# Three groups of transposes moved from TensorE to DMA, with a new order of the work, in an interleaved memory-transformer and gated-MLP kernel

## The chip, the cores and the metric

The kernel runs on one core of a Trainium2 chip. A core has five instruction streams that matter here: PE (TensorE, matmuls; its weight loads are shown apart as PEld), DVE (VectorE), ACT (ScalarE), POOL (GpSimd) and SP (SyncE, which issues all of this kernel's DMAs). The metric is the device time of one launch in microseconds (us). Before the change it is 1519.08 us, the median of three runs (1517.13, 1519.08, 1519.72).

## The reference

Input x has 2048 tokens of 448 numbers. Four layers are applied one after the other, each added to its input: A, B, A, B.

Layer A is attention with a recurrent memory. Its normalised input is cut into 64 segments of 32 tokens. Ahead of each segment stand 8 memory rows, so 40 rows are attended to at a time, by 16 heads of 256, with a mask that lets a token see the memory and the tokens up to itself. The first 8 rows of a segment's output are the memory of the next segment; this makes a chain of 64 steps that can't be done side by side.

```python
for s in range(n_seg):
    h = concat([mem, x[s*32:(s+1)*32]])          # 40 rows
    q, k, v = h @ Wq, h @ Wk, h @ Wv
    p = softmax(where(mask, q @ k.T * scale, -1e9))
    o = (p @ v) @ Wo
    mem, out_s = o[:8], o[8:]
```

Layer B is a gated MLP on the normalised rows: gate = x Wg, up = x Wu, h = relu(gate) · up, out = h Wd, with 1792 hidden numbers. The second A starts from the same initial memory and has the same weights as the first, and so have the two Bs.

## The kernel before

**Layout.** The tokens are worked on in 16 tiles of 128, four segments each. Wq and Wk are multiplied together ahead of time into A, and Wv and Wo into Bsb, so that a head's scores are h A h^T and its output is P h Bsb. All weights stay in SBUF. What flows between stages is bf16.

**The chain.** `chain(step)` does one memory step of both A layers at once: layer 1 runs seven steps (LAG) behind layer 0. Only the 8 memory rows of a segment go through it. Products with A (L885), turned on DVE (L1059, L1067), scores and softmax in `middle` (L1082 to L1100), P turned on PE (L1115) and copied to PTm, P times the rows (L1139, L1142, from HR), the product with Bsb (L926), and a split into two bf16 halves that puts the new memory rows back into mT, HT and HR. For layer 1 the rows for HR are four DMAs from Rsb on SP; for layer 0 they are copied.

**The riders.** In layer 1 the tokens of even tiles ride along in unused columns of the chain's matmuls, 16 of them a step (`ride`, and `third` near the end). Their softmax is a second call of `middle` with a mask, with its own Pr and PTr, of which there is one each. It is emitted behind the chain's step and its result is used by the next step's product. A rider's result goes by DMA from Rsb to Tsb, eight issues a step.

**The tokens.** `att_group` does a tile's tokens for a quarter of the heads, four calls a tile: products with A into Ug (L1228), scores (L1254), softmax on DVE and ACT (L1261 to L1267) into Px, two PE transposes (L1273) into a PSUM bank, one copy into PTx, P times the rows (L1139, L1142) into YT, and the product with Bsb (L1303). Layer 0 has all 16 tiles and layer 1 the eight odd ones: 96 calls. Px has two buffers, PTx one.

**The MLP.** `norm` normalises a tile's rows (L1159 to L1168) into xn and, for the MLP, turns them by four PE transposes (L1174) into a bank. From there one copy of 128x512 fills blocks 0 to 3 of G2, and two copies of 64x384 fill blocks 4 to 6 with the halves swapped. `glu_units` reads G2 in pairs of half-height matmuls (L1327), `glu_down` multiplies with Wd (L1346). There are 32 MLP tiles. The rows for layer A (`norm` with another destination) are turned the same way, into HT and HX.

**What sets the order.** The program is recorded as operations with their costs, and `_Sched` lays them out before anything runs. PE's order is written out: LINE lists, operation by operation, which of those not yet placed comes next, and PE does exactly that order. ORDER shifts the due times of parts of the work, which decides the order on the other engines. An operation waits on semaphores for what it reads; there is no other choice at run time. Each engine, SP among them, does its list in sequence. For a DMA the plan takes a cost on SP (750 or 640 ns), its bytes at 240 a nanosecond, and 1800 ns to land. A change of PE's tiling is planned at 94 ns (TURN). Where PE would stand idle long enough (L267), `filler` puts dummy matmuls (L1360) into a free PSUM bank.

Of the kernel before, what the change touches and what calls it, by code (L numbers as in the profile page):

```python
# [12 lines left out]
D = 448  # L13
# [5 lines left out]
L = SEG + M  # L19
# [13 lines left out]
ORDER = ("bpAIADoUQHoTkoMiV0AFwEKXLXJgtlHyqWXmIAyASPAYGXRWF0TArkrptiYIWoOAZasL0tFJGlTFY0Pedbealsyx0xoaZwia00qain0aZhAqaa"  # L33
         "cadkYaijdaUN0aD0m0aaUq0AqNQHxbPP0XcAhyv0bfDu0ZIrGH0UPaaaxbawMsAcXQyNBy0hi0mLLnTInmxTcmcobaXApXz0jagMaQLfnPpTIL"
         "HMxTAQTSZiNNblpydZg0geLAJizGtLa0jagUxTedmKDD0iU00msmturofpI0IAryFNTMkbTvuDpa0cls0MUtoc0ASOXN0DAs0FaRDazrtMsuoT"
         "0WNcIsHAPagayA0DOPTCQndFH0SANUPHki0MFvzaHuatOHNAbPqVt0qILltpAOehTTg00zngDSv0F0AaKNLAmrjWmTySi0muj0NXlaNd0KkAFJ"
         "TkhTraEYaAGBA0pDPTvfvtzKlo0oTAyaIsgQfHAye0jXsTgWNqGGXsAZadTaFYhmO00APvWovBKSASpAWILKnJPSlAaXUFk0xQMjLfnAXHQAKh"
         "tqfFLHPE0ieJ0wXdrkbWeTalAaoAbBwcdomWDzQPLNggtFrfiXWSsBOxTXKrAstuhHvQLCaZkaxNazRHeRhfqyLUHbrXTJgG0wJ0YEVDJTKnAV"
         "lC0PJXjpDrc0pD0ApoEmOmMwXxSREx0cxzoPOsmadeaLLAAj0piwNJ0lsyWbapNSJVVIsVOsihOZwYAW0jaRFtZbyCaqTaKNbJQTfIB0mZS0Cc"
         "WxgOQZcnsYWAoAITywNmqXZUhIPgkCkP0Jdz0ubAW0ZhAoPAcmjhqTtPaiVaJlb0KEBYgskpDe0DR0CWAAqQTsDKYTTAgjdedfcQPGPnAsAa0p"  # L40
         "avNPCvdomUwqVOJc0xauAvNdte00NPHjppXCUqsbyAAyNhifJMAXbzeWlwVjZXuELnDd0HVgTaAEafBwIEaRHujNotAXn00JAfBST0SeGqg0bi"
         "jwfrq0VssGFsaEjazUWQIpRMksFRCWhQNqSYNZMwWYXwgzxLmvPo0yhHRFerP0e0aIz0LUKmshQkGBgtIJulh0AAauQzacAadK0PyjGtjbaaaa"
         "aaAThZKZSaaaaaaaaaaaaaaaaaaawXLEBNvdaUYLxbEb")

SIGNS = "ABCDEFGHIJKLMNOPQRSTUVWXYZabcdefghijklmnopqrstuvwxyz0123456789+-*/=<>()[]{}.,:;!"
LINE = ("AEFAEDKLFHHDDEDEDMKIFGGEEDADCKJGFEEDDCCCJKIFGDCDCDMLCJAFEDEDCBBKIEGCCBBBBBKJ1DBGAEDBAAMAHOMCCBJBBCAAAdeAFbBMCA"
        "BWDVVADOCSCAPBbOABMfEAWKBVKJBBABBADYBARBAAVFBADVACNDACKBDPBADGGDNNDLEDEEDAFECAAAAAWAAAKARAAPHdAcGASAQAAAU~FBMA"
        "~CAhgA(ACdAAbA+aADXXXXDDAATEADDQPAAAALAAJJJAIIAHAGGABBDAABBAAAAAATMiAAXWdWKAaJJ~JALlAK~N~EKAAAEEAHDAZZGFCABFBS"
        "BBWQABOAAMMMAAKAJKKAzQJCIHHBGGGAFAHGADADJABBAAAAAACANBBYAXQAGIaISAHWAGAAARFDeEEAGCaZFFABBFBSBBQVAPBAAMMMAAKAJK"
        "K2AsQJCIHHBGGGAFoIHeBADEAACBBAEAAABCAAMBAYXQAJbbKTAhIAeAAAHERYADA--EiDpC6AEBB82DABEAxfEDuuuAAFrAEErqEmAlAlCAjo"  # L50
        "ShhKggg9BAfIdVACabaAAYAACAUZABSKAQQQDAANGOiPOgYBLMcrVMRAKKcKKKAgKDAHCCSFyyAfAPACsAARpBAn~DnnnD!EDAAiAhDjiDDAFA"
        "AcaAAZYC*BWAAAASSSAS0DQBSRAANOUAAALAJJDCHHHAHIGASGGAAOASACMBeVKBSBYBBBOFTAEAEDA.}Cut[CUC>A]pD/APCC999FAAK5A465"
        "lCCA1AA5AyCAwvmdtttBAb)FppBGnonEADDqjDDAmgCKeCdddCDbDDaaaZCPFWCbCALSARXAQQQTDZDDNAFAAI99EDGAAA3AA16jBzHyyyHyAW"
        "vALuuAsKAQpACOAlCBjnADhhhAAfBABAedbACACB4XAAAUATSmSSSASphBCAANAAaAKAlkDAbhIUmwUIISBAfTAFAAACKXBB1KKBBBFWFIBEAA"
        "><QEEC-CCCA7B-BH4AcBA000AZAxCwAxwCkBjUrBwBAonWmDBBBOhhhBBXfeBBddC9DbCgAZFXIWAVVVAAAVSpUU/n2SADRXAAPOWOBAMMMBOA"
        "KDJIJ54DVDGAAyADAv0DuMCsssABqACoppDNCFAAjJ>hhDAfDCAcccEcAAZABBYYAAATATpwSSAWsAQAPPPAAAMAaAKAdAArIUfATGGGaAPoAA"
        "DMMDALCAOBBBGZGYBIEB[[GKGACC/CA(ME9A8h777AA5BA65BbAi1zEAAXwAvukBBrrrsATYEnXmDnm9DRDjpDDDgDkeeDdddAAbcEbbBGBBXA"
        "DFaUASERAAPPPCRAAMA==CKuAIJA7HWW+4AN2M111MAYyBXAyxDOUDDqAAEvoBBmAlk,CBiiiAAhCAeABAccDACCXAAVAAZTASmSSSTAgnBAAA"
        "NAAZAAAjAIUAATdFRFFPRPAEAMACAJOBJTIBBBOWFBEFBA((EPDO/G)CCA9KAo6o5556CfCC1Aj00AADAAvC~BBUrrBquASoooCemAQnmQCBOB"
        "fBfBBAicAaaAZZZCAIWBXYXAHKSDSAAAPOCNRAMMMEAAKAIHA+9QPH6OAFb82FA0ZAyyyAfAvAAwvBKAJrxDoAAGmBk(kBKAhhhDhAgDCdAEAb"  # L60
        "aEDAAAAUAASnSuSSSASoACAAAALAZAJAkAAUHBBBVEEPhAXNdCCOLSYCAJBJcJBBBXJVBEASAC<=vFuE+CC=FABB4nBBBcAyA1AAvvv~GBAt~D"
        "AutsUAEpSuAAmdlDkkkBBiNBBfggEDeAAAbgCGYPXAEVVVBMBSUCRERRADgDBNTVBBLDAIIUCbCGGGPAAHFDDAgwwDNDAsABDIBnsAmNlllBLB"
        "iAJDfAffC}dCAiAaACAXAWA9AUUUAASARTSqAoRQBBOBNAMMMAALKAAeXjCiJVBVmeJIARrFTGdSAFaEE4OEEEAHZDACA][DACFC=AB)B-AA9L"
        "A7778AA5BAAA32bAAzC4AXwvdumtttlBuArqbtspFFnoZGAktqkFjEiiijEEiEfxFhhADDdIEibEEZFWhXWDE99UUUXAUCAKAPACOWWN7C6UdA"
        "ASXKRALPPPAPANBAAONAEIIAIAAGFFAEEEAADCABPAUGASAYAXDPJAACGGCAEBLFAEECGCFFCAGBBBBBAABCFAADAAABAAAAAA")
# [22 lines left out]
class _Sched:  # L88
# [12 lines left out]
    PE_END = 162.0  # L101
    ROWS = {"act": 122.0, "dve": 115.0}
# [92 lines left out]
    def schedule(self):  # L195
# [35 lines left out]
        while left:  # L231
# [34 lines left out]
            if e == "pe" and begun:  # L266
                n = int((t0 - free[e] - 300.0) * 0.8 / 190.0)  # L267
                room = [(t, b) for b, (t, _) in empty.items() if t is not None and t <= free[e]] if n > 0 else ()
                if room:
                    b = min(room)[1]  # L270
                    f = self.filler(n, b, empty[b][1], free[e], len(seq))
                    order[e].append(f)
                    seq.append(f)
                    mode = f.mode
# [11 lines left out]
            if o.dma:  # L286
                free[e] = t0 + c
                dma_free = max(dma_free, t0) + o.dma / 240.0
                o.end = dma_free + 1800.0
            elif e == "pe":  # L290
                t0 = max(t0, free[e] + turn)
                o.start = t0
                free[e] = t0 + c
                o.end = t0 + c + self.PE_END
            else:
                free[e] = t0 + (c - self.PIPE[e] if o.busy is None else o.busy)
                o.end = t0 + c
# [24 lines left out]
    def filler(self, n, bank, deps, start, seq):  # L322
# [3 lines left out]
        f.idx, f.engs, f.cost, f.eng, f.dma, f.touch, f.mode = -1, ("pe",), {"pe": n * 190.0}, "pe", 0, [], 0  # L326
        f.fn = lambda E, e: self.spin(E, bank, n)
        f.deps = {d: True for d in deps}
        f.prio, f.start, f.end, f.need_inc, f.seq, f.users, f.alloc, f.busy = (0, 9), start, start + n * 190.0, False, seq, [], (), None
# [152 lines left out]
class _Kernel:  # L482
# [39 lines left out]
    def alloc(self):  # L522
# [46 lines left out]
        self.PTx = sb("PTx", [128, 256])  # L569
# [14 lines left out]
        self.R0 = sb("R0", [128, 256])  # L584
# [90 lines left out]

    def weights(self):
# [76 lines left out]
        homes += [[("G2", g, v) for g in range(2) for v in range(3)]]  # L753
# [61 lines left out]
    def memory0(self):  # L815
# [3 lines left out]
        s.add("pool", 300, lambda E, e: E.memset(R[:, :], 0.0), w=[("R0", j) for j in range(10)])  # L819
        n = 0  # L820
        for j in range(4):
# [3 lines left out]
            for a, b in ((7, 0), *main):  # L825
# [3 lines left out]
              r=[("R0", j) for j in range(10)], w=["mT0"])  # L829
# [239 lines left out]
    def middle(self, act, m, row, col, P):  # L1069
# [44 lines left out]
        bp = self.bank("C", "G")  # L1114
        s.add("pe", 56, lambda E, e: E.matmul(bp.ap().bitcast(BF)[:, 0:128], lhsT=m["P"][:, :], rhs=self.ident[:, :], is_transpose=True),  # L1115
              r=[k_("P"), k_("P0"), k_("P1"), "ident"], w=[bp], alloc=[bp], **P)
        s.add(EV, ev_cost(128, fast=True), copy_any(m["PT"][0:104, :], lambda: bp.ap().bitcast(BF)[0:104, 0:128]), r=[bp], w=[k_("PT")], **P)
# [33 lines left out]
    def norm(self, t, dst):  # L1151
# [26 lines left out]
        if dst == "G":  # L1178
# [3 lines left out]
            s.add("pe", mm_cost(*[128] * 4), tr, r=xnk + ["ident"], w=[bk], alloc=[bk], room=[("G2", g, v) for v in range(3)])  # L1182
            s.add(EV, ev_cost(512, fast=True), copy_any(G[:, 0:4, :], pk), r=[bk], w=[("G2", g, 0)])
            for v, to, of in ((1, lo, up), (2, up, lo)):
                s.add(EV, ev_cost(384, fast=True), copy_any(G[to, 4:7, :], lambda of=of: pk()[of, 0:3]), r=[bk], w=[("G2", g, v)], at=1 + v)
# [16 lines left out]
    def att_group(self, l, t, g, bo):  # L1202
# [43 lines left out]
        T, P, PT, st = self.Tx[si], self.Px[si], self.PTx, self.stx[si]  # L1246
# [21 lines left out]
        bp = self.bank("G", "C")  # L1268
        Pf = P[:, :, :].rearrange("p g k -> p (g k)")

        def pt(E, e):
            for p in range(2):
                i = E.matmul(bp.ap().bitcast(BF)[:, 128 * p:128 * p + 128], lhsT=Pf[:, 128 * p:128 * p + 128], rhs=self.ident[:, :],  # L1273
                             is_transpose=True)
            return i
        s.add("pe", mm_cost(128, 128), pt, r=[("Px", si), "ident"], w=[bp], alloc=[bp], room=["PTx"])
        s.add(EV, ev_cost(256, fast=True), copy_any(PT[0:104, :], lambda: bp.ap().bitcast(BF)[0:104, 0:256]), r=[bp], w=["PTx"])

        for p in range(2):
# [4 lines left out]
            def yy(E, e, p=p, HR=HR, yb=yb):  # L1284
                for q in range(5):
                    for h in range(2):
                        r0 = 64 * h
                        i = self.y_part(E, yb[h].ap(), HR, r0, q, PT[r0:r0 + L, 128 * p:128 * p + 128], 128)
                return i
            hk = [q for h in range(2) for q in self.hr_keys(l, 4 * t + 2 * p + h)]  # L1290
            s.add("pe", mm_cost(*[128] * 3, 64, 64), yy, r=["PTx"] + hk, w=yb, alloc=yb, room=[("YT", yi, p, h) for h in range(2)], mode=2)
# [193 lines left out]
```

## Time and profile before

| what | value |
|---|---|
| median of the runs | 1519.08 us |
| the profiled execution's own time | 1519.32 us |
| its span, first to last instruction | 1517.4 us |
| TensorE clock granted | 0.999 |
| DVE STREAM_TRANSPOSE of the chain (L1059) | 280, 558 ns each |
| L1273, L1174, L1115: PE transposes | 192, 256, 136; 216 to 230 ns each |
| copies into PTx | 70 on ACT at 0.38 us, 26 on DVE at 0.29 |
| copies into PTr | 45 on ACT at 0.28 us, 21 on DVE at 0.22 |
| copies of 128x512 into G | 21 on ACT at 0.60 us, 11 on DVE at 0.42 |
| DMAs issued on SP | 1021 |

A time of one instruction is from its start to its end. On PE matmuls overlap, so busy times there are the union of such spans; a matmul's slot is read from the starts of neighbours. For a DMA, the row under SP is what the issue takes on SP; the landing comes later and shows only where something waited for it. L numbers are lines of the kernel before; in the changed kernel the same lines stand 5 to 10 lower down to the softmax of the tokens, and at the same place behind.

### The profile page before, as it was taken

The numbers are of one execution on the slowest core, as the hardware profiler recorded it, in microseconds if no ns is written. First come the engines' busy times: TensorE is split into PE (matmuls) and PEld (weight loads), VectorE is DVE, ScalarE is ACT, GpSimd is POOL, SyncE is SP. The second block draws the span as 40 slices with busy tenths as digits, with TensorE's granted clock in tenths as the row PEclk, the third lists the DMA queues.
The fourth block names the chain that finished last, engine by engine and source line by source line (L and its number), as shares of the span: only waits on it lengthen the run. The fifth ranks groups of instructions, "written<-read, shape, count | busy, mean of one in ns | idle before, by whom it ended". The sixth has DMA issues, their size and how long they took to land.

```text
span 1517.4 us, 82709 instructions
## 1 busy us (share of the span) xinstructions
PE 1491.6 (98%) x36998; PEld 1057.7 (70%) x36998; DVE 1175.1 (77%) x3594; ACT 884.9 (58%) x2392; POOL 116.5 (8%) x478
## 2 busy tenths in 40 slices
PE   8999999999999999999999999999999999999999
PEld 5557566666767776777767677677677777677776
DVE  6657677788878887787877887688787878788774
ACT  8776465555555656555665556556564556555543
POOL 1000000000000000000000000010000000000000
PEclk9999999999999999999999999999999999999999
DMA  8502100000000000000000000000000000000000
GB/s 240 171 25 78 41 7 11 11 9 8 9 4 12 11 8 14 4 18 4 18 4 9 14 8 14 4 17 5 17 5 8 14 8 15 5 8 8 11 5 14
DMA packets 60658, 34.08 MB, mean 22 GB/s; under 512 B 31744, under 2 KB 60176, under 8 KB 60304
## 3 DMA queue, kind: packets, MB, share of 16 engines
q1 hardware_dynamic: 60304, 28.80, 7.4%
q8 instruction: 291, 4.77, 1.4%
q14 instruction: 63, 0.52, 0.1%
HBM read 21.36 MB, written 1.84 MB: 15 GB/s over the span
## 4 chain that ended last, share of the span: by engine, by line
PE 90%; DVE 5%; ACT 2%; DMA 1%; issue 1%; SPq 0%; POOL 0%; DVEq 0%; POOLq 0%
PE psG L1228 16%; PE psG L1303 16%; PE psG L1327 11%; PE psC L926 11%; PE psC L885 8%; PE psG L1346 5%; PE psG L885 5%; PE psG L1139 3%; PE psG L716 3%; PE psG L1254 2%; PE psC L1082 1%; PE psG L703 1%; PE psC L1139 1%; PE psC L945 1%; PE psG L1174 1%; PE psG L1142 1%
## 5 line engine op out<-in xcount | busy, mean ns | idle before, releaser
L1228 PE MATMUL psG<-HT,A 64*128 64x128 bf16 x4900 | 287.7, 216 | 2.1 <-issue 1.0
L1303 PE MATMUL psG<-Bsb,YT 128*128 128x448 bf16 x1288 | 275.4, 352 | 0.4 <-DVE YT L425 0.4
L1228 PE MATMUL psG<-HX,A 64*128 64x128 bf16 x3675 | 267.5, 216 | 0.0
L1228 PEld LDWEIGHTS psG<-HT,A 64*128 64x128 bf16 x4900 | 235.3, 94 | 14.5 <-issue 6.0
L422 ACT ACTIVATE Ug<-psG 64x128 bf16<-64x128 f32 (+2 forms) x453 | 161.4, 377 | 62.3 <-PE psG L1228 49.7
L1228 PEld LDWEIGHTS psG<-HX,A 64*128 64x128 bf16 x3675 | 194.9, 94 | 0.2 <-issue 0.2
L1327 PE MATMUL psG<-G,glu 64*128 64x128 bf16 x6034 | 188.6, 216 | 0.5 <-issue 0.3
L926 PE MATMUL psC<-Bsb,YTm 128*32 128x448 bf16 x3640 | 184.6, 353 | 0.6 <-DVE YTm L425 0.2
L1327 PEld LDWEIGHTS psG<-G,glu 64*128 64x128 bf16 x6034 | 173.9, 94 | 11.5 <-issue 5.5
L1303 PEld LDWEIGHTS psG<-Bsb,YT 128*128 128x128 bf16 x1288 | 113.2, 97 | 93.4 <-issue 6.3
L1059 DVE STREAM_TRANSPOSE uT<-Usb 128x384 bf16<-128x384 bf16 x280 | 154.1, 558 | 5.2 <-ACT Usb L422 1.1
L885 PE MATMUL psG<-A,mT 64*32 64x448 bf16 x4060 | 143.8, 350 | 0.7 <-issue 0.7
L926 PEld LDWEIGHTS psC<-Bsb,YTm 128*32 128x32 bf16 x3640 | 91.3, 97 | 73.6 <-ACT YTm L422 2.1
L885 PE MATMUL psC<-A,mT 64*32 64x448 bf16 x3780 | 137.2, 350 | 1.7 <-issue 0.8
L422 ACT ACTIVATE YT<-psG 128x448 bf16<-128x448 f32 x244 | 124.6, 545 | 18.1 <-PE psG L1142 16.7
L934 ACT ACTIVATE Ohi<-psC 128x448 bf16<-128x448 f32 (+1 forms) x134 | 51.3, 383 | 127.1 <-PE psC L926 90.1
L425 DVE CAST Ug<-psG 64x128 bf16<-64x128 f32 (+2 forms) x238 | 99.5, 429 | 12.4 <-PE psG L1228 9.2
L1332 ACT ACTIVATE hG<-psG 128x512 bf16<-128x512 f32 (+1 forms) x124 | 67.5, 545 | 66.0 <-PE psG L1327 63.6
L935 DVE TENSOR_TENSOR Olo<-psC,Ohi 128x448 bf16<-128x448 f32 (+1 forms) x134 | 56.5, 422 | 63.8 <-ACT Ohi L934 62.8
L885 PEld LDWEIGHTS psC<-A,mT 64*32 64x32 bf16 x3780 | 69.7, 92 | 48.8 <-DVE mT L425 2.1
L1333 DVE TENSOR_TENSOR hG<-hG,psG 128x512 bf16<-128x512 bf16 (+1 forms) x121 | 74.4, 619 | 29.9 <-ACT hG L1332 28.8
L1346 PE MATMUL psG<-glu,hG 128*128 128x448 bf16 x434 | 95.2, 352 | 0.0
(228 smaller groups left out, 2841.0 us busy)
## 6 DMA issues: line engine op xcount, KB each, us to landing
HR<-xn SPq DMA_DIRECT2D x128, 32.0 KB
Tsb<-Rsb SPq DMA_DIRECT2D x256, 1.5 KB
Tsb<-Rsb SPq DMA_DIRECT2D x256, 2.0 KB
Bsb<-in_A_Wq_dram SPq DMA_DIRECT2D x8, 384.0 KB
Bsb<-in_A_Wk_dram SPq DMA_DIRECT2D x8, 384.0 KB
HR<-Rsb SPq DMA_DIRECT2D x126, 1.5 KB
HR<-Rsb SPq DMA_DIRECT2D x126, 2.0 KB
X<-in_A_x_dram SPq DMA_DIRECT2D x16, 112.0 KB
```

Source lines behind the costliest of these rows:

```text
L422: return E.activation(out, i, ACT.Copy, scale=1.0 if scale is None else scale)
L425: return E.tensor_copy(out, i)
L885: i = E.matmul(ub[v].ap()[32 * j:32 * j + 32, 0:D], lhsT=self.mT[rw, WHERE[b], first:first + 32], rhs=cols, start=(b == 0), stop=(b == 6), ...
L926: x = E.matmul(bo.ap()[32 * j:32 * j + 32, 0:D], lhsT=self.YTm[:, q, :], rhs=self.Bsb[:, chunks[q], :], start=(i == 0), stop=(i == 13), ti ...
L1059: self.s.add("dve", 578, lambda E, e, out=out, hh=hh: E.transpose(out, heads[hh]), r=[("Usb", 2 * half + v) for v in range(2)], w=[f"uT{ha ...
L1139: return E.matmul(ps[:, n * q:n * q + n], lhsT=HR[rows, 128 * q:128 * q + 128], rhs=PT, start=True, stop=True, tile_position=(b, 0))
L1228: i = E.matmul(ub[v].ap()[:, 128 * n:128 * n + 128], lhsT=self.A[rw, b, a0:a0 + 128], rhs=HT[rw, WHOLE[b], :, 0:SEG] if CROSS[b] is None e ...
L1303: i = E.matmul(bo.ap()[:, 0:D], lhsT=YT[:, c, :], rhs=self.Bsb[:, 14 * g + c, :], start=(g == 0 and c == 0), stop=(g == 3 and c == 13))
L1327: i_ = E.matmul(two[v].ap()[:, 128 * c:128 * c + 128], lhsT=self.Wgu[rw, b, f0:f0 + 128], rhs=G[rw, WHOLE[b] if CROSS[b] is None else 4 + ...
L1332: s.add("act", 170 + 0.833 * N, lambda E, e, dst=dst, z=two[0], N=N: E.activation(dst, z.ap()[:, 0:N], ACT.Relu), r=[two[0]], w=[("hG", i, ...
L1333: s.add("dve", dv_cost(N), lambda E, e, z=two[1], N=N, dst=dst: E.tensor_tensor(dst, dst, z.ap()[:, 0:N], ALU.mult), r=[two[1]], w=[("hG", ...
L1346: i_ = E.matmul(bk.ap()[:, 0:D], lhsT=hG[:, c, :], rhs=self.Wd[:, c, :], start=(c == 0), stop=(c == NFC - 1))
```

## The change

Three groups of PE transposes are replaced by DMAs that transpose on the way, from SBUF to SBUF, issued on SP:

- the tokens' P: one DMA of 128x256 from Px into PTx, in place of two PE transposes and a copy. PTx gets a second buffer; R0, which holds the initial memory at the start, now lies in it.
- the riders' P: one DMA of 128x128 from Pr into PTr. The chain's own P stays on PE.
- the MLP's rows: two DMAs, of 128x384 and 128x128, from xn into blocks 0 to 3 of G2. The two copies with the halves swapped read G2 instead of PSUM.

That makes 96 + 66 + 64 = 226 DMAs. The rows of layer A are turned on PE as before.

In the plan a transposing DMA costs 900 ns on SP and four times its bytes, and every DMA lands 2400 ns after its bytes, where it was 1800. ORDER and LINE are new throughout, so that all engines' lists differ from end to end. Dummy matmuls are also placed ahead of the first chain step now, as 128-column products of the identity.

```diff
+    LAND = 2400.0
...
-            if e == "pe" and begun:
-                n = int((t0 - free[e] - 300.0) * 0.8 / 190.0)
+            if e == "pe" and (begun or done > 1):
+                ns = 190.0 if begun else 56.0
+                n = int((t0 - free[e] - 300.0) * 0.8 / ns)
...
-                o.end = dma_free + 1800.0
+                o.end = dma_free + self.LAND
...
-        self.PTx = sb("PTx", [128, 256])
+        self.PTx = [sb(f"PTx{i}", [128, 2, 128]) for i in range(2)]
...
-        self.R0 = sb("R0", [128, 256])
+        self.R0 = self.PTx[1].rearrange("p a b -> p (a b)")
...
+    def turned(self, dst, src, nbytes, r, w, prio=None):
+
+        self.s.add("sp", 900, lambda E, e: E.dma_start(dst, src, transpose=True), r=r, w=w, dma=4 * nbytes, prio=prio)
...
-        bp = self.bank("C", "G")
-        s.add("pe", 56, lambda E, e: E.matmul(bp.ap().bitcast(BF)[:, 0:128], lhsT=m["P"][:, :], rhs=self.ident[:, :], is_transpose=True),
+        if m["mask"] is not None:
+            self.turned(m["PT"][:, :], m["P"][:, :], 32768, [k_("P"), k_("P0"), k_("P1")], [k_("PT")], prio=P["prio"])
+            bp = None
+        else:
+            bp = self.bank("C", "G")
+        if bp: s.add("pe", 56, lambda E, e: E.matmul(bp.ap().bitcast(BF)[:, 0:128], lhsT=m["P"][:, :], rhs=self.ident[:, :], is_transpose=True),
...
-            s.add("pe", mm_cost(*[128] * 4), tr, r=xnk + ["ident"], w=[bk], alloc=[bk], room=[("G2", g, v) for v in range(3)])
-            s.add(EV, ev_cost(512, fast=True), copy_any(G[:, 0:4, :], pk), r=[bk], w=[("G2", g, 0)])
+            self.turned(G[:, 0:3, :], xn[:, 0:KZ].rearrange("t (k q) -> t k q", k=3), 98304, [("xn", i, 1)], [("G2", g, 0)])
+            self.turned(G[:, 3, :], xn[:, KT:KW], 32768, [("xn", i, 0), ("xnt", i)], [("G2", g, 3)])
             for v, to, of in ((1, lo, up), (2, up, lo)):
-                s.add(EV, ev_cost(384, fast=True), copy_any(G[to, 4:7, :], lambda of=of: pk()[of, 0:3]), r=[bk], w=[("G2", g, v)], at=1 + v)
+                s.add(EV, ev_cost(384, fast=True), copy_any(G[to, 4:7, :], G[of, 0:3, :]), r=[("G2", g, 0)], w=[("G2", g, v)], at=1 + v)
...
-        s.add("pe", mm_cost(128, 128), pt, r=[("Px", si), "ident"], w=[bp], alloc=[bp], room=["PTx"])
-        s.add(EV, ev_cost(256, fast=True), copy_any(PT[0:104, :], lambda: bp.ap().bitcast(BF)[0:104, 0:256]), r=[bp], w=["PTx"])
+        self.turned(PT[:, :, :], P[:, :, :].rearrange("r (p g) k -> r p (g k)", p=2), 65536, [("Px", si)], [k_("PT")])
...
-            for _ in range(n):
-                i = E.matmul(self.psum[bank][:, 0:D], lhsT=self.A[:, 0, 0:128], rhs=self.A[:, 1, 0:D], start=True, stop=True)
+            w, x = (self.A[:, 0, 0:128], self.A[:, 1, 0:D]) if ns > 100 else (self.ident[:, :], self.ident[:, :])
+            for _ in range(n):
+                i = E.matmul(self.psum[bank][:, 0:x.shape[1]], lhsT=w, rhs=x, start=True, stop=True)
```

## The prediction, made before the changed kernel was run

> **What bounds the kernel now.** I read the page's busy times first, then the table of stretches, to see whether TensorE is full everywhere or only on average.
>
> ```profile
> span 1517.4 us, 82709 instructions
> ...
> PE 1491.6 (98%) x36998; PEld 1057.7 (70%) x36998; DVE 1175.1 (77%) x3594; ACT 884.9 (58%) x2392; POOL 116.5 (8%) x478
> ...
> PE 90%; DVE 5%; ACT 2%; DMA 1%; issue 1%; SPq 0%; POOL 0%; DVEq 0%; POOLq 0%
> ```
>
> ```profile
> 0.00:100.00 100.00, 91.99 (x1330) 55.86 (x1331) 65.56 (x151) 79.98 (x149) 11.19 (x36) 0.98 0.54 159
> 100.00:200.00 100.00, 94.43 (x2446) 66.35 (x2448) 68.05 (x204) 57.31 (x155) 6.62 (x25) 1.00 0.19 52
> 300.00:400.00 100.00, 97.58 (x2524) 68.92 (x2518) 81.31 (x259) 58.20 (x170) 8.20 (x34) 1.00 0.05 9
> 400.00:600.00 200.00, 199.69 (x5154) 143.59 (x5153) 163.33 (x516) 115.82 (x328) 16.30 (x69) 1.00 0.05 10
> 1000.00:1200.00 200.00, 199.98 (x5160) 144.86 (x5138) 164.85 (x517) 117.32 (x336) 15.46 (x65) 1.00 0.05 11
> ```
>
> In the table the third number of a line is PE's busy time, and DVE's and ACT's follow PEld's. The reader is to see that from 400 us on PE stands still for 0.0 to 1.4 us in 200, while DVE and ACT have a fifth and two fifths free. PE's idle time, 1517.4 − 1491.6 = 25.8 us, lies almost wholly before 400 us. So from there on a PE instruction taken out is worth its slot, and work taken from DVE or ACT is worth nothing by itself.
>
> What a slot is worth is not the 219 ns that a matmul is shown with, since they overlap. The timeline of PE near the end shows starts:
>
> ```profile
> 1485.75 0.27 PE L1273 MATMUL psG<-ident,Px 128*128 128x128 bf16 x2
> 1485.95 1.74 PE L1327 MATMUL psG<-G,glu 64*128 64x128 bf16 x56
> ...
> 1489.03 0.28 PE L1273 MATMUL psG<-ident,Px 128*128 128x128 bf16 x2
> 1489.15 0.92 PE L1303 MATMUL psG<-Bsb,YT 128*128 128x448 bf16 x4
> ...
> 1492.27 0.39 PE L1174 MATMUL psG<-ident,xn 128*128 128x128 bf16 x4
> 1492.49 0.73 PE L1303 MATMUL psG<-Bsb,YT 128*128 128x448 bf16 x3
> ```
>
> Two transposes hold the next work up by 0.12 us and four by 0.22, so 0.056 each. Before L1327, which uses half-height tiles, it is 0.20: the change of tiling adds some 0.09.
>
> For the new transfers the nearest rows are the plain SBUF-to-SBUF ones: the issue times on SP (min/median/max in ns), and two landings on the chain in order of time (start, us from issue to landing).
>
> ```profile
> L674 SPq DMA_DIRECT2D HR<-Rsb x252: 685/686/1573, 206.2 to 1469.9; - x126
> L674 SPq DMA_DIRECT2D HR<-xn x128: 507/590/1610, 42.5 to 1417.5; - x128
> ```
>
> ```profile
> 321.46 3.60 DMA HR<-xn
> 1335.77 1.87 DMA HR<-xn
> ```
>
> ```profile
> 677.84 2.99 SPq L674 DMA_DIRECT2D HR<-Rsb  x4
> 680.88 6.20 SPq L674 DMA_DIRECT2D Tsb<-Rsb  x8
> 697.74 2.85 SPq L674 DMA_DIRECT2D HR<-Rsb  x3
> ```
>
> The last fence is SP's timeline over one step: 9.2 us of issues, and the next step's first 19.9 us after this one's. SP has 10.7 us free in a step.
>
> **The change, part by part.** The sum goes against the profiled run's 1519.3 us (span 1517.4 and 1.9 around it; the median of the runs, 1519.08, is 0.2 below).
>
> *Taken from PE.* Counted in the two lists of instructions: 128 transposes of normalised rows (L1174, 32 MLP tiles of four), all 192 of the tokens' P (L1273) and 66 of the riders' (L1115, which keeps 70 for the chain). 386 × 0.056 = 21.6 us. Changes of tiling could have gone with them, at 0.09 each; but the new order has 634 against 632, so nothing. Weight loads ran beside matmuls before and count for nothing.
>
> *Taken from ACT and DVE.* 96 copies into PTx, 66 into PTr, 32 of 128x512 into G. On ACT 70 × 0.38 + 45 × 0.28 + 21 × 0.60 = 52 us, on DVE about 26 × 0.29 + 21 × 0.22 + 11 × 0.42 = 17 us. PE's work covers both engines, so I count nothing; if PE's cover were gone (the stretches before 400 us) a copy's 0.3 to 0.6 us would be a gain. The two half copies per MLP tile remain, now out of SBUF behind the landing (0.36 on DVE, 0.49 on ACT as read from PSUM). They go into the lag below.
>
> *Added to PE.* Dummy matmuls, which the planner puts where it expects PE idle: 62 of 448 columns and 5 of 128 against 33 of 448. A 448-column matmul takes 0.19 us from start to start, so 29 more are 5.5 us (the five narrow ones 0.3, left out). They stand in 28 separate places against 10, and L268 of the new code leaves 0.3 us of each such gap unfilled: 18 × 0.3 = 5.4. Together 10.9 us of PE time without useful work. Bounds: 0, if these gaps were only late in the plan and the dummies fall into idle that is there anyway, and 12.3, since the line also fills no more than four fifths of the rest. I take 10.9 since dummies occupy PE whether or not the gap comes. Eight of the 28 places stand after 400 us, where before had none.
>
> *Added to SP.* 226 transposing DMAs, 3.4 a step. At 0.59 to 0.69 us (plain issues) they are 133 to 156 us; the plan allots 0.9. All fits in the 10.7 us per step, so no cost by itself. What it costs is order: SP runs its list in sequence, and a transpose that waits for DVE's P holds up whatever stands behind it. In the new list 68 of the 226 are directly followed by a row piece for HR, 46 of them by one from Rsb, which the second chain's next step reads.
>
> *The new wait.* Before: P, PE transpose, copy, use. After: P, SP's turn, transfer, use. Pairing through the trace the end of P (L1267; L1112 for riders; the last normalised piece, L1168, for MLP rows) with the first matmul that uses its transpose gives the time that is there today: tokens 1.1 us least, 4.7 at the tenth of the cases, 10.1 median; riders 1.8, 4.1, 13.5; MLP rows 2.2, 2.9, 20.2. A transfer's lag is bounded by the rows at 1.87 and 3.60. With today's order, summing all shortfalls, a lag of 2 us would cost 2.0 us, of 3 us 13.8, of 4 us 32, of 6 us 81. The new order is spaced wider: on an axis of PE slots, from a token group's scores to the first use of its P, the least distance grows from 4.2 to 5.8 us and the twentieth's from 6.2 to 8.1. So I shift the lags by 1.6 us: a lag of 3.6 costs 2 us, of 4 us about 6. Below 3.6, nothing. I take 4 us of cost for a lag between these: the upper landing row, since a 128x384 transpose moves three times HR's 32 KB, plus a fraction for SP's turn. A gain is excluded: the wait only replaces a shorter one.
>
> *Last tile.* Its rows can't come earlier than the adds behind the last L1303. Normalisation took from 1498.12 to 1501.08; with 3.6 of lag and 0.5 of half copies that is 7.7 us after the add. The order puts the previous tile's whole MLP there: 196 matmuls of L1327 in pairs and 14 of L1346, 5.5 + 2.6 = 8.1 us. Covered, by a hair; each us of lag beyond is a us.
>
> Sum: −21.6 + 10.9 + 4 = −6.7, so 1512.6.
>
> The trace has a transpose's slot at 0.056 us. The Trainium skill, in "VectorE: DVE Perf Modes", The three transpose paths, gives 390 ns for TensorE and 1309 for the DMA crossbar, and advises TensorE where PSUM will do as destination. By that rule this change moves work the wrong way: 386 × 0.92 = 355 us if every one stood on the path, an estimate from that page; by the lags measured above hardly any does, so as a mechanism it is the late case below and has its chance; the page's 1.3 us would take my 4 us off and give 1508.6.
>
> **The rivals.**
> - *The gain is eaten, no change (15%).* If the wider spacing was bought with gaps that are longer than the dummies show, or the second chain's rows come late by SP's order, −6.7 becomes 0: 1519. For it: 18 new gaps. Against it: PE's 77%-busy suppliers get 69 us of work less.
> - *The full slot is kept (10%).* The dummies fall into idle time that before had as well, and nothing lands late: 1519.3 − 21.6 = 1497.7. For it: 25.8 us of idle are there. Against it: the dummies behind 400 us.
> - *Late landings, slower (33%).* Place: PE's fixed order at the first use of PTx, PTr and G. If P to landing takes over about 4.4 us, SP's turn included, the shortfall (today's order at 2.8, near 11 us) passes the 10.7 that is left of the gain, and the sign turns. At 6 us the sum at 4.4 of today's order applies, about 41 us; as one stall gives all later ones air, half to all of it: 1529 to 1550. For it: eight Tsb issues in a row take 6.2 us, and a transpose behind them waits that long. Against it: the order was laid with later landings than before.
> - *SP becomes the bound (within the last).* From 10.7 / 3.4 = 3.1 us of issue each, five times a plain one; at 4 us a step grows by 2.9 us, over 60 steps 174 us: 1680.
>
> **How the numbers follow.** My forecast (faster, 1505 to 1516) has 42%, the full slot 10%, no change 15%, late landings 33%. Three runs of before spread by 0.17%, so 0.2% (3 us) is what can be told from no change. Faster 0.52, same 0.15, slower 0.33. The range runs from 1500, between forecast and full slot, to 1540, the middle of the late case: left out are some 5% below and 13% above. The forecast's own range is 1505 to 1516.
>
> **What will show it.** Right: 386 PE transposes gone, PE busy near 1475 us in a span near 1511, PE still full from 400 us on but for a few gaps at L1361. Lag: the time from a transposing issue to its landing, and PE's weight loads of L1148 (PTx, PTr) and L1327 waiting for DMA; over 10 us of that in total speaks for the late case. SP: issues above 3 us. Wrong altogether, if the chain's share of DMA or of DVE grew by tens of us.

## The result, and the profile after

The kernel after takes 1523.13 us (median of 18 runs, 1516.45 to 1526.80); the kernel before, run between them on the same chip, 1518.58 (18 runs). The ratio is 1.0029, with a 95% interval of 1.0020 to 1.0038: slower by 0.29%, some 4.4 us, where 1512.6 and "faster" had been forecast. The profiled run took 1524.53 us.

The page of the kernel after, busy times and the shares of the chain that ended last:

```profile
span 1522.8 us, 82109 instructions
...
PE 1483.1 (97%) x36646; PEld 1043.4 (69%) x36646; DVE 1157.2 (76%) x3534; ACT 845.5 (56%) x2258; POOL 117.6 (8%) x478
...
PE 84%; DVE 8%; DMA 4%; ACT 2%; SPq 2%; issue 1%; POOL 0%; DVEq 0%
```

PE is busy for 8.5 us less, and the span is 5.4 us longer: its idle time went from 25.8 to 39.7 us. In the chain PE lost six points, to DVE (from 5 to 8%), DMA (1 to 4%) and SP's queue (0 to 2%). The table of stretches says where (the third number of a line is PE's busy time). First two stretches of the kernel before that were not shown above, then the kernel after:

```profile
800.00:1000.00 200.00, 198.74 (x5223) 147.12 (x5228) 156.49 (x484) 116.09 (x330) 15.83 (x65) 1.00 0.05 10
...
1400.00:1500.00 100.00, 99.56 (x2332) 71.16 (x2330) 71.71 (x216) 49.23 (x128) 2.48 (x11) 1.00 0.04 9
```

```profile
400.00:600.00 200.00, 199.11 (x5134) 143.20 (x5120) 162.55 (x503) 115.77 (x325) 16.11 (x68) 1.00 0.09 20
600.00:800.00 200.00, 197.66 (x5096) 140.81 (x5092) 157.86 (x487) 108.69 (x303) 16.08 (x67) 1.00 0.09 19
800.00:1000.00 200.00, 195.13 (x5074) 141.75 (x5069) 157.08 (x486) 106.17 (x297) 16.17 (x65) 0.99 0.09 20
1000.00:1200.00 200.00, 196.05 (x4965) 138.69 (x4958) 151.18 (x475) 111.79 (x307) 15.47 (x64) 1.00 0.09 20
...
1400.00:1500.00 100.00, 94.24 (x2190) 65.43 (x2185) 68.16 (x203) 41.49 (x107) 2.41 (x11) 1.00 0.08 17
```

PE's idle time grew from 1.3 to 4.9 us between 800 and 1000 us, from 0.0 to 4.0 in the next 200, and from 0.4 to 5.8 between 1400 and 1500; between 1200 and 1400 it hardly changed (1.4 and 1.9). With the slot lengths that the code gives its matmuls (`mm_cost`), PE's stream can be split into slots and all that lies beyond them (changes of tiling, stalls): slots fell from 1404.1 to 1388.3 us, which is the 386 transposes less the new dummies, and what lies beyond rose from 108.8 to 129.9.

What SP issues, in the kernel after (min/median/max in ns), and rows of the waits for DMA by waiting engine and line (us in total, times, longest). The first row of the waits is of the kernel before, the others are of the kernel after:

```profile
L679 SPq DMA_TRANSPOSE PTx<-Px x96: 1169/1212/2389, 120.5 to 1495.0; - x96
L679 SPq DMA_TRANSPOSE PTr<-Pr x66: 1097/1144/2292, 206.6 to 1466.4; - x66
L679 SPq DMA_TRANSPOSE G<-xn x64: 1117/1232/2596, 156.4 to 1508.9; - x64
L675 SPq DMA_DIRECT2D Tsb<-Rsb x512: 685/686/1383, 224.3 to 1494.3; - x171
```

```profile
DVE X L1393 <- DMA Tsb<-Rsb: 2.1, 3, 0.8
```

```profile
DVE X L1394 <- DMA Tsb<-Rsb: 11.6, 5, 3.8
ACT G L423 <- DMA G<-xn: 9.5, 8, 2.2
DVE Pr L1117 <- DMA PTr<-Pr: 6.4, 3, 3.6
...
DVE Px L1276 <- DMA PTx<-Px: 3.3, 2, 2.0
DVE G L426 <- DMA G<-xn: 3.1, 5, 0.9
...
PE psG L1327 <- DMA G<-xn: 1.8, 3, 1.0
PEld psG L1148 <- DMA PTx<-Px: 1.4, 1, 1.4
```

A transposing issue holds SP for 1.1 to 1.2 us, twice a plain one, and SP's issues add up to 1009 us where they were 687. The second view holds the surprise: PE, of which the prediction spoke, waits little for the new DMAs directly. DVE and ACT wait, in places the prediction had not priced: for Tsb, an old transfer (2.1 us in all before); for P's buffers, which the program doesn't let be written while a DMA still reads them; and at the half copies behind G's landing.

Paired in the trace from the end of P, SP reaches the tokens' transpose after a median of 1.8 us, 5.2 at three quarters and 9.0 at nine tenths of the cases. From the start of its issue it then lands after 2.4 us (median; nine tenths under 3.7). P to landing is 4.6 us at the median, 7.9 and 11.8 behind.

One place shows the mechanism from end to end. SP's timeline of the kernel after, then DVE's, then PE's (start, us, [idle before <- releaser]):

```profile
666.51 2.50 SPq L679 DMA_TRANSPOSE G<-xn  x2
669.05 1.24 SPq L679 DMA_TRANSPOSE PTx<-Px  x1
670.34 2.49 SPq L675 DMA_DIRECT2D HR<-xn  x4
672.87 2.16 SPq L679 DMA_TRANSPOSE PTx<-Px  x1
675.08 2.98 SPq L675 DMA_DIRECT2D HR<-Rsb  x4
678.10 1.72 SPq L679 DMA_TRANSPOSE PTr<-Pr  x1
679.87 4.34 SPq L675 DMA_DIRECT2D Tsb<-Rsb  x6
684.26 1.18 SPq L679 DMA_TRANSPOSE PTx<-Px  x1
685.48 1.43 SPq L675 DMA_DIRECT2D Tsb<-Rsb  x2
```

```profile
688.00 0.58 DVE L1394 TENSOR_TENSOR X<-Tsb,X 128x384 bf16<-128x384 bf16 x2 [2.50 <-DMA Tsb<-Rsb]
688.50 0.62 DVE L1310 TENSOR_TENSOR X<-psG,X 128x448 bf16<-128x448 f32 x1
689.03 0.23 DVE L1109 TENSOR_TENSOR Tr<-psC,mask 128x80 f32<-128x80 f32 x1
```

```profile
689.32 0.23 PE L1237 MATMUL psG<-HT,A 64*128 64x128 bf16 x1 [1.45 <-DVE Tr L1109]
```

SP has no gap for 20 us. A step's eight Tsb issues stand behind five transposes and are cut in two by a sixth, so the last pair is issued at 685.48. DVE's list stops 2.50 us at X for them. Behind X in that list stands Tr, which empties a PSUM bank, and PE waits for that bank. No DMA is named at PE, though one is the cause.

### The profile page after: what moved, and what is told of

It reads as the page before. It is cut to its first block, busy times and chain, and to the rows that moved or that the text cites. A ratio compares the mean times of both kernels' runs of the same rounds, so it can differ in the third digit from the quotient of the medians.

```text
span 1522.8 us, 82109 instructions
## 1 busy us (share of the span) xinstructions
PE 1483.1 (97%) x36646; PEld 1043.4 (69%) x36646; DVE 1157.2 (76%) x3534; ACT 845.5 (56%) x2258; POOL 117.6 (8%) x478
## 4 chain that ended last, share of the span: by engine, by line
PE 84%; DVE 8%; DMA 4%; ACT 2%; SPq 2%; issue 1%; POOL 0%; DVEq 0%
PE psG L1303 15%; PE psG L1237 14%; PE psG L1327 10%; PE psC L931 10%; PE psC L890 9%; PE psG L1346 5%; PE psG L890 3%; PE psG L721 3%; PE psG L1148 3%; PE psG L1263 2%; PE psC L1087 1%; PE psC L1148 1%; PE psG L708 1%; SPq L675 1%; DVE uT L1064 1%
## 5 line engine op out<-in xcount | busy, mean ns | idle before, releaser
L1237 PE MATMUL psG<-HT,A 64*128 64x128 bf16 x4828 | 282.8, 216 | 4.0 <-DVE Tr L1109 1.4
L1303 PE MATMUL psG<-Bsb,YT 128*128 128x448 bf16 x1344 | 283.7, 353 | 0.0
L423 ACT ACTIVATE Ug<-psG 64x128 bf16<-64x128 f32 (+2 forms) x425 | 151.7, 380 | 78.6 <-PE psG L1237 64.9
L1303 PEld LDWEIGHTS psG<-Bsb,YT 128*128 128x128 bf16 x1344 | 117.9, 97 | 103.0 <-issue 7.4
L931 PE MATMUL psC<-Bsb,YTm 128*32 128x448 bf16 x3472 | 176.9, 355 | 2.3 <-DVE YTm L426 1.8
L890 PE MATMUL psG<-A,mT 64*32 64x448 bf16 x3976 | 158.1, 350 | 0.0
L890 PE MATMUL psC<-A,mT 64*32 64x448 bf16 x3864 | 155.7, 350 | 0.5 <-DVE mT L426 0.3
L890 PEld LDWEIGHTS psC<-A,mT 64*32 64x32 bf16 x3864 | 79.5, 92 | 57.5 <-DVE mT L426 5.9
L426 DVE CAST Ug<-psG 64x128 bf16<-64x128 f32 (+2 forms) x275 | 109.2, 408 | 12.0 <-PE psG L1237 7.2
L890 PEld LDWEIGHTS psG<-A,mT 64*32 64x32 bf16 x3976 | 83.5, 93 | 17.1 <-DVE mC L426 0.4
```

The costliest lines, as they stand in the source:

```text
L423: return E.activation(out, i, ACT.Copy, scale=1.0 if scale is None else scale)
L426: return E.tensor_copy(out, i)
L890: i = E.matmul(ub[v].ap()[32 * j:32 * j + 32, 0:D], lhsT=self.mT[rw, WHERE[b], first:first + 32], rhs=cols, start=(b == 0), stop=(b == 6), ...
L931: x = E.matmul(bo.ap()[32 * j:32 * j + 32, 0:D], lhsT=self.YTm[:, q, :], rhs=self.Bsb[:, chunks[q], :], start=(i == 0), stop=(i == 13), ti ...
L1237: i = E.matmul(ub[v].ap()[:, 128 * n:128 * n + 128], lhsT=self.A[rw, b, a0:a0 + 128], rhs=HT[rw, WHOLE[b], :, 0:SEG] if CROSS[b] is None e ...
L1303: i = E.matmul(bo.ap()[:, 0:D], lhsT=YT[:, c, :], rhs=self.Bsb[:, 14 * g + c, :], start=(g == 0 and c == 0), stop=(g == 3 and c == 13))
```

## The experiments

Each ratio is to the kernel before, run in the same five rounds on the same chip, with its 95% interval in brackets; 0.1% is 1.5 us. The experiments ran on three chips, so two of them are compared by their ratios. Each starts from the kernel after unless it says otherwise, with the same lists on all engines.

### PE freed from the new waits

```diff
-                if not self.needs(o, d):
+                if not self.needs(o, d) or (o.eng == "pe" and d.late in FREE):
...
-        G, hG = self.G2[g], self.hG[i]
+        G, hG = self.G2[g] if "G2" not in FREE else self.fix, self.hG[i]
```

and the same for PTx and PTr; `self.fix` is a part of A, and `late` marks the transposing DMAs and the half copies. In the first kernel all three are freed, in the second the tokens' P alone.

> The kernel after, with the same order on every engine and the same transfers issued, but PE reads a fixed region of the weights in place of PTx, PTr and G, and so waits neither for a transposing transfer nor for the half copies behind one. Left out of the computation: what is read there (the tokens' and riders' P of the attention, the MLP's normalised rows) is other data. The kernel after took 1.0029 of the kernel before. Theory A (the loss is made by transposes that land late, above all by their turn in SP's list): 11 to 16 us go, 1507 to 1511 us, ratio to the kernel before 0.992 to 0.995. Theory B (the landings cost little by themselves; the new order is poorer for other reasons, the chain's DVE steps and the rows that SP brings later): 1518 to 1522, ratio 1.000 to 1.002. Theory C (29 more dummy matmuls eat the gain): like B, within 3 us of 1523.

> As the kernel with all three freed, but only PTx, the tokens' P, is replaced by fixed data and not waited for; PTr and G are as in the kernel after. Left out of the computation: the tokens' P. Theory A: directly at PTx stand 6.5 us of the 13 us that PE waits at these three after 400 us, so half of what goes with all three freed, 1515 to 1518. Theories B and C: 1521 to 1523.

Measured: 1518.53 us, ratio 0.9997 (0.9984 to 1.0011) with all three, and 1519.96, 0.9999 (0.9985 to 1.0012) with the tokens alone. So what PE itself waits for at these places is worth 0.32%, 4.9 us. (This prices late landings and late P together: PE freed in this way doesn't wait for P itself either, which it had to before the change too.) That is neither theory A, which expected 11 to 16, nor B's nothing at all. Freeing the tokens alone gives as much as all three, so riders and rows cost nothing measurable here; the expected half was a miss. Some 15 us still lay between this kernel and what its fewer slots promise (1519.03 of the kernel before on that chip, less 15.8, is 1503.2).

### The riders' rows left out, and the control

```diff
-                self.dma(to, of, 2048, r=[rk], w=[("Tsb", q, o, v)])
+                self.dma(to, of, 2048, r=[rk], w=[("Tsb", q, o, v)]).off = True
```

`off` takes the DMA out of SP's list after the plan is made, and Tsb is set once to a constant. The control has the same edit in the kernel before.

> The kernel after with the same orders, but the 512 small transfers Tsb<-Rsb aren't issued; Tsb is a constant. Left out of the computation: the riders' rows of the second chain's tiles. This takes some 300 us of issuing from SP and all work of the transposing transfers stays. Theory A, if SP's turn makes them late: 8 to 13 us go, 1510 to 1515, and the median from the end of a token's P to the start of its issue falls from 1.8 us to under 1. Theory A, if the transfers themselves make them late: 1519 to 1523. Theory B in the form 'rows that SP brings later': 1512 to 1518. Theory C: 1523.

> Control: the kernel before, with the 512 small transfers Tsb<-Rsb left out in the same way (Tsb a constant; left out of the computation are the riders' rows of the second chain's tiles). In the kernel after, leaving them out took the ratio to the kernel before from 1.0029 to 0.9924. Theory S (it is the 311 us of transposing issues that make SP's list tight, and only there do the small transfers cost something): within 3 us of the kernel before, 1516 to 1519. Theory R (the small transfers cost the same with either form of transpose): 8 to 12 us go here as well, 1507 to 1511.

Measured: 0.9924 (0.9910 to 0.9939) from after, 1507.96 us, some 16 us less, where 8 to 13 had been expected; 0.9978 (0.9969 to 0.9987) from before, 1516.69. The same 512 small issues are worth 1.05% in the kernel after and 0.22% in the kernel before. The wait from P's end to the tokens' issue fell to a median of 0.5 us. So the trouble hangs on SP's list, which the transposes crowd.

### The dummies

```diff
+        self.seq = [o for o in self.seq if o.idx >= 0]
         for o in self.seq:
             for d in o.deps:
```

> The kernel after without its dummy matmuls; everything else stands in the same order and the output is the same. Theory C (dummies occupy PE whether or not the gap comes, 67 of them): all that they occupy goes, about 12 us, 1511, if the gaps are never there; by the step of the prediction (62 x 0.19 us against the gaps that they fill) 5 us go where the gaps don't come, 1518. Theories A and B: the dummies fill time in which PE waits anyway, within 2 us of 1523, or slower if PE's granted clock falls in the gaps.

Measured: 1529.55 us, 1.0076 (1.0053 to 1.0100), slower than the kernel after by 0.47%. The mean granted clock of the profiled run is 0.993 against 0.997. Stretches of the kernel without dummies, and the same two of the kernel after (the number behind POOL's is the granted clock):

```profile
220.00:240.00 20.00, 16.24 (x479) 10.94 (x462) 12.85 (x38) 11.26 (x29) 2.40 (x11) 0.91 0.07 13
240.00:260.00 20.00, 17.53 (x433) 11.40 (x428) 16.11 (x51) 9.61 (x28) 2.26 (x9) 0.91 0.09 19
```

```profile
220.00:240.00 20.00, 18.78 (x537) 12.68 (x523) 14.12 (x40) 11.56 (x29) 2.68 (x11) 1.00 0.08 14
240.00:260.00 20.00, 18.69 (x473) 12.56 (x468) 17.50 (x61) 11.90 (x38) 2.41 (x9) 1.00 0.10 21
```

Theory C falls: the dummies cost nothing on balance, and without them PE's clock drops. Over all runs the clock's mean is 0.992 against 0.999. An estimate from these two gives up to 10 us of PE time lost by the clock (0.007 of 1525), where the kernel lost 7; so up to 3 us of the dummies' own slots may have been a cost that this run hides. The trace has three gaps on PE there, at 223.6, 225.4 and 249.3 us, of 1.28, 1.46 and 1.82 us. The Trainium skill, "TensorE: Matmul & The Clock Gate", Part 1, has the array's clock halved after an idle window of about 3.4 us; that a quiet PE loses clock agrees with these rows, the length does not, as no gap there reaches 2 us. A gap's length doesn't settle it in this trace either: a gap of 2.22 us at 1414.9 left the clock at 1.00 in the stretch from 1414 to 1434 us.

### The transposes not issued at all

From the kernel in which PE is freed of all three:

```diff
         o = self.s.add("sp", 900, lambda E, e: E.dma_start(dst, src, transpose=True), r=r, w=w, dma=4 * nbytes, prio=prio)
+        o.off = True
```

> As the kernel in which PE reads fixed data in place of PTx, PTr and G and waits for none of them, and the 226 transposing transfers aren't issued either, so SP has its other transfers alone. Left out of the computation: what those tiles hold. With the transfers issued this gave 1518.5 us. Theory S (the transposes cost most by delaying what stands behind them on SP, row pieces and Tsb): 10 to 15 us below that, 1504 to 1509. Theory A (they cost by their own late landing): 1516 to 1519, as nothing waited for them there already. Theory B (the order is poorer in itself): 1516 to 1519.

Measured: 1502.38 us, 0.9881 (0.9866 to 0.9895), more of a gain than theory S expected. Issuing 226 DMAs that PE does not wait for costs 1.16%, 17.6 us. SP's timeline at the step shown above, and DVE at its X:

```profile
666.42 2.45 SPq L691 DMA_DIRECT2D HR<-xn  x4
669.02 2.98 SPq L691 DMA_DIRECT2D HR<-Rsb  x4
672.05 6.16 SPq L691 DMA_DIRECT2D Tsb<-Rsb  x8
```

```profile
682.44 0.58 DVE L1412 TENSOR_TENSOR X<-Tsb,X 128x384 bf16<-128x384 bf16 x2 [0.52 <-issue]
```

The eight Tsb issues end at 678.2 and X waits for no DMA. PE's time beyond its slots is 107.4 us here, 108.8 in the kernel before. So the new order is not poorer in itself, at least where PE doesn't have to wait for P, and theory B falls as the main cause.

### Which part of it

Three kernels divide the 17.6 us. In the first, DVE and ACT wait for no transposing DMA either: these read A in place of P and xn, and the half copies read `self.fix`.

```diff
-                if not self.needs(o, d) or (o.eng == "pe" and d.late in FREE):
+                if not self.needs(o, d) or d.late in FREE and o.eng in ("pe", "dve", "act"):
...
-        o = self.s.add("sp", 900, lambda E, e: E.dma_start(dst, src, transpose=True), r=r, w=w, dma=4 * nbytes, prio=prio)
+        o = self.s.add("sp", 900, lambda E, e: E.dma_start(dst, self.still(src), transpose=True), r=[*r, *FIX], w=w, dma=4 * nbytes, prio=prio)
```

The second has, in place of each transposing DMA, two plain ones of 8x64 elements; the third is the first with X adding a part of A and not waiting for Tsb.

> As the kernel in which PE reads fixed data in place of PTx, PTr and G (1518.5 us), and further: the transposing transfers read a fixed region of the weights in place of P and of the normalised rows, and the half copies read a fixed region in place of G, so that DVE and ACT wait for no transposing transfer either. All 226 transfers are still issued, at the same places of SP's list, once P is there. Left out of the computation: what those tiles hold. Without the issues this form gave 1502.4. Theory T (the turn and time on SP delay the row pieces and Tsb, whatever waits for the transposes): 1513 to 1518. Theory W (the new waits of DVE and ACT, in order, for P's buffers and for G: 19 us together in the kernel after): 1503 to 1508.

> As the kernel in which nothing waits for the transposing transfers, with each of the 226 replaced by two plain transfers of 1 KB, about 0.6 us of issue each, so that SP is taken for the same time without the transposes' work in the DMA engines. Left out of the computation as there. Theory T by SP's time: within 3 us of the kernel with the transposing transfers that nothing awaits. Theory T by the DMA engines' work: 1502 to 1505, as without the issues.

> As the kernel in which no engine waits for a transposing transfer (1516.2 us, 0.9977 of before), and DVE's add into X doesn't wait for Tsb either: it reads a fixed region of the weights. All transfers are issued as before. Left out of the computation: what those tiles and Tsb hold. Without the 226 issues the first form gave 0.9881. Theory D (SP's lost time reaches PE through DVE's list, which stops at X for Tsb, 13.9 us in six stops): two thirds or more of the difference goes, ratio 0.988 to 0.991, 1501 to 1506. Theory H (it reaches PE through the row pieces for HR, which the chain and the tokens read): within 0.1% of 0.9977, 1514 to 1517.

Measured: 0.9977 (0.9966 to 0.9987), 1516.16 us, with nothing awaiting the transposes; 0.9961 (0.9946 to 0.9975), 1513.62, with small DMAs in their place; 0.9913 (0.9898 to 0.9928), 1506.78, with Tsb not awaited besides.

Theory W falls: the new waits of DVE and ACT, 22 us when added up, are worth 0.20% to the end, 3.0 us, which is only just clear of the intervals. Theory T holds: the issues alone, which nobody awaits, cost 0.96%, 14.6 us. Small DMAs that hold SP for nearly as long (305 us in all, where the transposes took 319) cost 0.80%, so it is SP's time; what the transposes' work in the DMA engines adds, 0.16%, can't be told from nothing with these intervals. The Trainium skill, "Trainium Kernel Development and Optimization", Key Constraints, says that all queues share the same 16 DMA engines and that issuing from several saves the issue time only; these runs agree that the issue time is what counted.

SP's time has two parts that these runs keep together: the issues themselves, and the stops at a transpose whose P isn't there yet. In the kernel after SP stands still ahead of 68 of the 226 transposes, 156 us in all, and a stop of that kind could hold up what is queued behind it. The traces settle it for Tsb. From the row written to Rsb to the last Tsb issue of its step takes 8.8 us on average before the change and 10.5 after it. Of the added 1.7 us, 1.5 are transposes being issued and 0.03 are stops at them. So it is the issues that make Tsb late.

Two thirds of the 14.6 us (0.64%, 9.7 us) reach PE through DVE's stop at X for Tsb, at the lower edge of what theory D expected. In the kernel with nothing awaiting the transposes it is nearly all that DVE waits for DMA:

```profile
DVE X L1407 <- DMA Tsb<-Rsb: 13.9, 6, 4.5
...
DVE xn L1188 <- DMA HR<-xn: 2.2, 1, 2.2
```

The last third, 0.32%, is not shown. The row pieces for HR come later too (source to issue at most 3.0 us without the transposing issues, 5.9 with them), but a run with those alone freed was not made.

The same cut in the kernel after as it is had said little:

> The kernel after with all transfers issued, but DVE's add into X reads a fixed region of the weights in place of Tsb and doesn't wait for the small transfers. Left out of the computation: the riders' rows there. Theory S in the form that SP's time is what counts: 1520 to 1523, since SP issues as much as before. Theory R' (late Tsb holds up DVE's list, which waits 11.6 us there, and so PE): 1509 to 1515.

Measured: 1.0004 (0.9991 to 1.0016), 1520.13 us. Only 0.25% goes, not 0.64. A likely reason, which no run separates, is that the transposes' own late landings then stop the same engines a little later. What one wait is worth depends on which others are gone.

### The small transfers on another queue

```diff
-                self.dma(to, of, 2048, r=[rk], w=[("Tsb", q, o, v)])
+                self.dma(to, of, 2048, r=[rk], w=[("Tsb", q, o, v)]).put = "act"
...
+        for o in self.seq:
+            o.eng = o.put or o.eng
```

For POOL the same with "pool", and with 16 semaphores of their own for these DMAs. All of the computation is done. The last kernel is the one before with the move to POOL.

> The whole computation of the kernel after, with the 512 small transfers issued from ACT's queue in place of SP's, at the place that their turn in the plan gives them. Some 300 us of issuing leave SP and come to ACT, which is busy for 845 us. Theory S: SP's relief is worth the 11 to 15 us that leaving the transfers out gave, but ACT's list stops for a round of eight issues (5 us) where PE waits for its copies; 1510 if those waits are covered, 1525 or more if not. Theory A by the transfers' own landing: 1523 or more.

> The whole computation of the kernel after, with the 512 small transfers Tsb<-Rsb issued from POOL's queue in place of SP's, at the place that their turn in the plan gives them. Leaving them out gave 1508.0; POOL is busy for 8% of the span. If SP's relief is what counts and POOL issues them within some 12 us of a step: 1508 to 1512, faster than both kernels. If POOL's issue is slow enough to hold up its copies into HT, which the chain waits for: 1525 or more.

> Control: the kernel before, with the 512 small transfers Tsb<-Rsb issued from POOL's queue in place of SP's; the whole computation. In the kernel after the same move took the ratio to the kernel before from 1.0029 to 0.993. With the small transfers left out altogether the kernel before came to 0.9978. If the move is only worth something where SP is crowded: 0.997 to 1.000, 1514 to 1519, and so the DMA transposes with the small transfers on POOL beat it by 0.4% or more. If it helps either kernel alike: 0.993 or less.

Measured: on ACT 1529.12 us, 1.0056 (1.0040 to 1.0073); on POOL 1508.68, 0.9930 (0.9917 to 0.9943); before with POOL 1517.52, 0.9977 (0.9965 to 0.9988). The issues, and PE's costliest wait with ACT:

```profile
L679 ACTq DMA_DIRECT2D Tsb<-Rsb x512: 695/696/1584, 223.4 to 1499.9; - x171
```

```profile
PEld psC L1128 <- DVE Pm L1109: 15.5, 27, 1.4
```

```profile
L689 POOL DMA_DIRECT2D Tsb<-Rsb x512: 544/559/696, 222.9 to 1472.1; - x171
```

On ACT eight issues take 5.6 us of the list that also has the chain's exponentials, and PE waits 15.5 us for the P behind those (6.8 in the kernel after). On POOL they take 4.5 us of a list that is 8% full. That version beats the kernel after by 1.0% and the kernel before by 0.7%, and the kernel before gains 0.2% by the same move. So with SP relieved, the whole change (transposes by DMA, with the new order) is worth 0.47% (0.9930 / 0.9977, from two comparisons), 7.1 us.

## Why the prediction was wrong

The ratios from the kernel after down to the one without the issues, each step taking one cause away, put a price on every term:

| term | predicted, us | measured, us |
|---|---|---|
| PE's slots, dummies and gaps | −21.6 + 10.9 | −18.1 (0.9881) |
| waiting at PE for the landings | +4 | +4.9 (0.9997 to 1.0029) |
| DVE and ACT waiting for the transposes | 0 | +3.0 (0.9977 to 0.9997) |
| SP's time | 0 | +14.6 (0.9881 to 0.9977) |
| sum | −6.7 | +4.4 |

The sum comes out because each price is the difference of two neighbouring ratios. The prices depend on the order in which the causes are taken away, as Tsb showed, and the first two rows are mixed: where PE was freed of the landings it was freed of waiting for P as well.

- **"All fits in the 10.7 us per step, so no cost by itself"** is the step that failed. It cost 14.6 us. Total time was the wrong measure. SP works its list in sequence and its work comes in bunches: HR's pieces and Tsb stand behind one event of the chain, transposes behind others, and each added 1.2 us moves all that is queued. The prediction saw the order ("holds up whatever stands behind it", the row pieces from Rsb) and then gave it no price. It also missed the main victim: Tsb, for which DVE stopped 2.1 us before, was nowhere in the sum, and it carries two thirds of the cost. This term decides the sign.
- **"Plus a fraction for SP's turn"** was mis-sized, within a term that came out. 4 us of cost at PE came out near the 4.9, but that is luck: the landing took 2.4 us from the issue, not 3.6, while "a fraction for SP's turn" was 1.8 at the median and 5.2 at three quarters. With the 4.6 us that P took to land at the median, the prediction's own curve (today's order at 3.0) gives 13.8 us.
- **DVE and ACT at nothing.** What the copies taken away were worth, no run shows by itself. The new waits in these engines' lists, for P's buffers until the DMA has read them and at the half copies, were left out of the sum, which put the half copies into the lag at PE: 3.0 us.
- **The dummies** were mis-sized. 5.5 us of their slots are in PE's stream, but the 5.4 for unfilled gaps did not show: time beyond slots was 107.4 without the transposing issues, 1.4 less than before. (PE waits for no P there; no run tells what such gaps cost where it does.) And "PE time without useful work" left out a use: without them the clock fell.
- **The rivals.** Late landings had the right sign and the wrong place: the stops at PTx, PTr and G decide 4.9 us, and the median of 4.6 from P to landing, past the 4.4 named as the point of turning, is no proof of it: 4.9 of the 22.5 us between the kernel after and the one without the issues are lost there. "The second chain's rows come late by SP's order", named under no change, was the nearest to the mechanism; it didn't name Tsb, and it stopped at no change. SP as the bound was wrong: it is busy for 1009 of 1523 us. It hurts at two thirds full.
- **The rule of 390 against 1309 ns** (the Trainium skill, "VectorE: DVE Perf Modes", The three transpose paths) pointed the way that the result went, but not for its reason: with the small transfers on POOL the same DMA transposes gain 0.47%. Neither figure is what a transpose cost here: a landing is 2.4 us from the issue, and what is paid is 1.1 to 1.2 us of SP.
- **Readings.** PE's 25.8 us of idle lie less before 400 us than "almost wholly" says: 18.7 of them do, and 2.9 are at the end. The last tile's 7.7 us are 7.1 by the times given (1498.12 to 1501.08, 3.6 and 0.5). Neither changes the sum.

## What to carry to other kernels

A queue that works in sequence is priced by what stands behind each added issue, not by its free time: follow who reads the next few transfers, and which engine's list stops there. The engine that waits may be two steps from the cause, so look for an old wait that has grown as well as for new ones. Before giving up on such a change, look for a queue with room: in this kernel, against leaving them out, the same 512 small transfers cost 1.05% on SP, 1.32% on ACT and 0.06% on POOL.

## What the runs showed of the hardware

- A transposing DMA from SBUF to SBUF holds SP for 1.14 us (128x128), 1.21 (128x256) and 1.23 (G's two, 128x384 and 128x128), and lands 2.4, 2.4 and 2.7 us after the start of its issue (medians). Size hardly matters between these; the plain DMAs for HR and Tsb, of 32 KB and less, take 0.59 to 0.69 us and land after 1.8 to 1.9.
- The same small DMA takes 0.69 us to issue on SP, 0.70 on ACT and 0.56 on POOL, where it counts as busy time (POOL went from 8 to 26% busy).
- In the kernel without dummies two stretches of 20 us that hold PE gaps of 1.3 to 1.8 us had a mean granted clock of 0.91; one with a gap of 2.22 us stayed at 1.00.
